# Key masks on VectorE, clears after the first norms, output sums on VectorE or GpSimd, and a planner that counts late instruction blocks

## The chip, the core and the metric

The kernel runs on one core of a Trainium2 chip, as one program. The core has five engines with an instruction queue each: TensorE (PE in the profile), ScalarE (ACT), VectorE (DVE), GpSimd (POOL) and SyncE (SP). The loading of weights into TensorE has a row of its own (PEld). The metric is the device time of one execution in microseconds.

## The reference

Two layers, each made of an attention A and a linear attention B on a residual stream of 2048 tokens by 512, 32 heads of 16. A works in four segments of 512 tokens: causal softmax attention inside a segment, plus a read from a memory that collects the keys and values of earlier segments.

```python
# A, for each segment s
p = softmax(q @ k.T * scale + causal_mask)
a_dot = p @ v
a_mem = (phi(q) @ M) / (phi(q) @ z + 1e-6)      # phi(t) = t+1 if t>0 else exp(t)
o = g * a_mem + (1 - g) * a_dot                 # g = sigmoid(beta), by head
M, z = M + phi(k).T @ v, z + sum(phi(k))
# B, for the whole sequence
phi(t) = concat(softmax(t @ w_phi), softmax(-t @ w_phi))
o = (phi(q) @ (phi(k).T @ v)) / (phi(q) @ sum(phi(k)) + 1e-6)
# twice:
x = x + A(layernorm(x)) @ wo_A
x = x + B(layernorm(x)) @ wo_B
```

## The kernel before

**A recorded program and a planner.** The kernel does not write out its order. Each operation is recorded in a graph with its reads and writes, a planned duration on each engine that may do it, and the tiles that it opens. `forward` then walks through time: whenever an engine is free it takes the ready operation of the highest priority. The result is a fixed order for each engine. Priorities come from twelve backward and forward passes for each of six rules, and then from a list of random moves, `STEPS`, each a seed that shifts the priority of some operations (`moved`). An engine works through its queue strictly in order; each instruction waits on semaphores for what it needs. Durations in the plan are constants in the code; a matmul of c columns is planned at c/2.4 + 2.5 ns.

**The two-engine rule.** Operations marked `port=True` on VectorE are not planned while POOL computes, and POOL does not start while such an operation runs. An operation with two entries in its table, such as `{"dve": (350.0, fn), "pool": (2900.0, fn)}`, may go to either engine.

**Instruction blocks in the plan.** `fetched` counts TensorE's instructions in blocks of `BLOCK = 256` (the first after `FIRST = 193`). Each pair of matmuls counts 4, two weight loads and two matmuls. When the end of a block is reached, the next may be used `FETCH = 3250` ns after the last one began; TensorE is planned to stand until then. The transfers of large inputs are planned one after another at 200 GB/s (`dfree`).

**Start.** `setup` records the loads. Four 128 KB loads of X and the raw weights wq and wk come first; then beta and w_phi on POOL. The loads of wv, of X for tokens 512 to 1023 and of wo are held until the norm of tile 3 (`gate = self.xnop[3]`), the rest (X, w_qkv of B, wo of B) until the norm of tile 7. POOL makes constants and clears: `pP`, the four tiles for diagonal probabilities, are zeroed in part (L879), the last column of the two value tiles `pV` is set to 1 (L881). VectorE clears `pQ2` (L877), held by the gate too. `ln` is the norm: statistics and their sum on VectorE (L918, L919), the inverse root on ScalarE for the first four tiles (L922, L924) and on POOL for the others (L926, L928), and the normed tile on VectorE (L939).

**Projections of A** (`a_proj`). For each half of the heads (`hp`) TensorE makes K and Q in PSUM, ScalarE or VectorE copies them to `KT` and `QT`. The key tile `KD` of `pK` is KT times a mask of 0 and 1 by partition, in two halves (L1028): 2 layers, 4 segments, 2 halves of heads and 2 parts make 32 masks. In the first segment of the first layer the queries too are masked (L1051, tiles `pQ0` and `pQ1`); elsewhere a DMA moves them. wv is scaled by the gate in eight operations on VectorE or POOL (L862, `WA_v`). wq and wk are permuted in sixteen (L871).

**Attention of A** (`a_att`). For each tile of 128 tokens, scores on TensorE (`pQ,pK` and, on the diagonal, `far,II`), exponentials on ScalarE (L651, to `p` and `pP`), products with the values (`pU`, `pV` with `p`, `pP`), division on VectorE (L697, L1173). From the second segment on, the memory part and the softmax part of the output are summed (L1177, 24 sums).

**B.** `b_keys` collects keys, `b_query` makes the output for each tile: a copy by ScalarE, a product with the inverse denominators (L1346, `nmul`), and the sum of the two signs (L1353, 26 sums; the other six tiles sum on TensorE). `out_proj` then transposes the sum by a DMA on SP's queue (`p<-p`), multiplies by wo, adds X on TensorE and copies to X (L659 or L660). In the second layer each tile is stored, from POOL's or SP's queue (L668).

Of the kernel before, what the change touches and what calls it, by code (L numbers as in the profile page):

```python
# [9 lines left out]
ALU = mybir.AluOpType  # L10
# [85 lines left out]
BLOCK, FIRST, FETCH, EXTRA = 256, 193, 3250.0, 0.126  # L96
# [6 lines left out]
class Graph:  # L103
# [143 lines left out]
    def forward(self, prio, pools, rule):  # L247
# [35 lines left out]
        issued, edge, begun = 0.0, float(FIRST), -1e9  # L283

        def fetched(dur, count):
            nonlocal issued, edge, begun
            count += EXTRA
            while issued + count >= edge:
                at = now + dur * (edge - issued) / count
                late = max(0.0, begun + FETCH - at)  # L290
                dur += late
                begun = at + late
                edge += BLOCK
            issued += count
            return dur
# [37 lines left out]
        while len(order) < n + fillers:  # L333
            while ev and ev[0][0] <= now + 1e-9:
                _, kind, i = heapq.heappop(ev)
                o = ops[i]
# [268 lines left out]
class Kernel:  # L605
# [402 lines left out]
    def a_proj(self, L, s):  # L1008
# [6 lines left out]
        for hp in range(2):  # L1015
# [8 lines left out]
            for m in range(2):  # L1024
                def fn(e, KT=KT, KD=KD, m=m, raw=raw):
                    dst = KD.t[:].rearrange("p (t x c) -> p t x c", x=4, c=64)
                    dst = dst[:, :, 0::3] if m else dst[:, :, 1:3]
                    return e.tensor_scalar(dst, KT.t[:].rearrange("p (t x c) -> p t x c", x=2, c=64), self.MK[:, 0 if raw else 1, m:m + 1], None, op0=ALU.mult)  # L1028
                self.g.op({"dve": (350.0, fn), "pool": (2900.0, fn)}, [KT, R("MK0") if raw else R("MK1")], [KD[m]], label="KD", port=True)
# [88 lines left out]
    def a_att(self, L, s, i):  # L1118
# [57 lines left out]
        if s >= 1:  # L1176
            v(lambda e: e.tensor_tensor(o.t[:], o.t[:], tmp.t[:], ALU.add), 335, [o[0], o[1], tmp[0], tmp[1]], [o[0], o[1]], label="oadd", port=True)  # L1177
# [113 lines left out]
    def b_query(self, L, c, store):  # L1291
# [38 lines left out]
        for tt in range(4):  # L1330
# [20 lines left out]
            if not pair:  # L1351
                half = lambda Tm, k: Tm.t[:].rearrange("p (b s c) -> p b s c", b=2, s=2)[:, :, k]
                v(lambda e, Tm=Tm, o=o, half=half: e.tensor_tensor(o.t[:].rearrange("p (b c) -> p b c", b=2), half(Tm, 0), half(Tm, 1), ALU.add),  # L1353
                  335, [Tm], [o], label="nadd", port=True)
# [3 lines left out]
    def build(self):  # L1358
# [9 lines left out]
        for L in range(2):  # L1368
            if L == 0:
                lnA(0, 0)  # L1370
                gate = self.xnop[3]
                for o in self.loads[self.early:self.second] + list(self.pQ.init.values()):
                    o.deps.add(gate)
# [44 lines left out]
def basep(ap):  # L1418
# [17 lines left out]
    1030000018, 1030000077, 1030000092, 1030000099, 1030000166, 1030000168, 1030000222, 1030000289, 1030000308,  # L1436
    1030000326, 1030000342, 1030000389, 1030000420, 1030000560, 1030000645, 1030000784, 1030000851, 1030000966,
    1030000984, 1030001009, 1030001690, 1030002205, 1030002291, 1030002301, 1030002323, 1030002439, 1030002527,
    1030002554, 1030002594, 1030002678, 1030002767, 1030002827, 1030002858, 1030003072, 1030003159, 1030003333,
    1030003714, 1030004121, 1030004204, 1030004671, 1030004934, 1030005425, 1030005496, 1030005653, 1030005764,  # L1440
    1030005994, 1030006207, 1030006544, 1030006744, 1030007011, 1030007046, 1030007069, 1030007218, 1030007220,
    1030007536, 1030008641, 1030008687, 1030008730, 1030009186, 1030009359, 1030009713, 1030009775, 1030009783,
    1030009816, 1030010053, 1030010635, 1030010656, 1030011598, 1030011826, 1030012430, 1030012462, 1030013373,
    1030013471, 1030013815, 1030014294, 1030014816, 1030014962, 1030015673, 1030017494, 1030017518, 1030017657,
    1030018904, 1030019905, 1030022035, 1030200092, 1030200096, 1030200172, 1030200329, 1030200464, 1030200971,
    1030201489, 1030201640, 1030202974, 1030203521, 1000400311, 1000402731, 1000403746, 1000404182, 1010600052,
    1010600600, 1010600903, 1010602519, 1010603776, 1010603875, 1020801005, 1020801937, 1020803898, 1031000849,
    1031002190, 1031003326, 1031004518, 1031201021, 1031202491, 1031202719, 1031202940, 1021400652, 1021400802,
    1021401184, 1021401558, 1021401865, 1021402577, 1021402781, 1021402889, 1021402967, 1021403407, 1031600163,
    1031601117, 1031601674, 1031601919, 1031602223, 1031602684, 1031602829, 1011800463, 1011801166, 1011801985,  # L1450
    1011802229, 1022000655, 1022002114, 1022002161, 1022002512, 1022002519, 1022002841, 1032201850, 1032202263,
    1032202919, 1012400450, 1012400549, 1012400881, 1012401973, 1012802802, 1013002895, 1013202988, 1033401154,
    1033403481, 1023603166, 1033803193, 1004001904, 1004003605, 1004400376, 1004400634, 1004600426, 1004601442,
    1034803444, 1025000113, 1025000301, 1025000392, 1025000954, 1025001054, 1025002108, 1035201603, 1035202380,
    1025601217, 1025601345, 1005800575, 1036000223, 1036001385, 1036002574, 1036201585, 1036201657, 1026401420,
    1016600059, 1016600512, 1016600897, 1016601902, 1036800336, 1036800865, 1036800917, 1036801080, 1036801719,
    1036801832, 1036802798, 1017001663, 1017002043, 1017002740,
# [41 lines left out]
```

## Time and profile before

| what | value |
|---|---|
| median of four runs | 531.06 us (528.14, 530.99, 531.13, 531.29) |
| the profiled run | 528.14 us; its span, first to last instruction, 526.4 us |
| TensorE clock granted, mean | 0.990 |
| key masks L1028 on POOL | 21, median 2862 ns, 62.0 us |
| key masks L1028 on VectorE | 11, median 478 ns, 5.2 us |
| sums L1177 and L1353 on VectorE | 24 of 418 ns and 26 of 414 ns, 20.8 us |
| POOL's inverse roots L926 and L928 | 60 of 338 ns and 60 of 602 ns |
| idle of POOL before L926, for the statistics L919 | 291.0 us |

Busy times of engines overlap, so they do not add up to the span. A clock below 1 means that TensorE was granted fewer cycles. "Idle before, releaser" names what ended an engine's wait. L640 is the line of the helper that issues nearly all matmuls, L651 that of ScalarE's operations: there one goes by the tiles. DMA transposes of a tile are issued on SP's queue and take 2.7 us (median) from issue to landing.

### The profile page before, as it was taken

Reading aid. Unit: us, or ns where it says so; the run is one execution under the profiler, and the core shown is the slowest. Engines: PE = TensorE matmul, PEld = TensorE weight load, DVE = VectorE, ACT = ScalarE, POOL = GpSimd, SP = SyncE. Lnnn points to the kernel's source line nnn. Section 1 sums busy time; section 2 is a strip of 40 time slices with the busy share of each in tenths; the row PEclk is TensorE's granted clock in tenths of the full one; section 3 lists DMA queues with packets and bytes.
Section 4 is the critical chain, followed back from the end, with each engine's and each line's share of the span. In section 5 each row is a group of like instructions: output and inputs, shape, how many; then the busy total and the mean of one; then the engine's idle time right before and its main releaser. Section 6 shows DMA issues by size and latency. Waiting matters only on the chain.

```text
span 526.4 us, 26401 instructions
## 1 busy us (share of the span) xinstructions
PE 474.9 (90%) x12182; PEld 320.9 (61%) x12182; DVE 423.7 (80%) x851; ACT 446.3 (85%) x555; POOL 144.0 (27%) x198
## 2 busy tenths in 40 slices
PE   7975998899989899999898989998989989999896
PEld 3353765565667676555756666665666656665674
DVE  6983899889978976886989879888887797877771
ACT  4784999889889899876998889999889998877894
POOL 6870571050450010000342281720041000010022
PEclk9997899999999999999999999999999999999999
DMA  6259345515223032000044445353112211100366
GB/s 191 52 148 199 64 92 92 92 37 92 44 39 70 14 44 34 12 2 2 21 66 103 92 101 97 77 74 59 33 34 54 54 23 33 24 14 2 44 137 128
DMA packets 90335, 34.11 MB, mean 65 GB/s; under 512 B 76752, under 2 KB 89072, under 8 KB 90224
## 3 DMA queue, kind: packets, MB, share of 16 engines
q1 hardware_dynamic: 88624, 27.68, 28.6%
q0 software_dynamic: 1600, 4.74, 3.1%
q8 instruction: 95, 1.56, 1.3%
q14 instruction: 16, 0.13, 0.1%
HBM read 6.32 MB, written 2.10 MB: 16 GB/s over the span
## 4 chain that ended last, share of the span: by engine, by line
PE 56%; ACT 18%; DMA 10%; DVE 10%; issue 3%; POOL 2%; SPq 0%; DVEq 0%
PE D L640 56%; ACT p L651 11%; DMA p<-p 7%; ACT pP L651 4%; POOL pK L1028 2%; DMA pX<-p 2%; DVE pT L1271 1%; DMA pK<-in_A_wv_dram 1%; DVE p L1173 1%; DVE X L1206 1%; DVE p L660 1%; DVE stats L918 1%; DVE pS L1251 1%; ACT X L659 1%; DMA X<-in_A_x_dram 1%
## 5 line engine op out<-in xcount | busy, mean ns | idle before, releaser
L651 ACT ACTIVATE p<-D 128x1024 bf16<-128x1024 f32 (+1 forms) x292 | 284.4, 1021 | 37.5 <-PE D L640 35.1
L640 PE MATMUL D<-pQ,pK 64*128 64x256 bf16 (+1 forms) x1356 | 118.3, 262 | 13.0 <-ACT pP L651 4.3
L651 ACT ACTIVATE pP<-D 128x768 bf16<-128x768 f32 x128 | 101.5, 822 | 15.1 <-PE D L640 13.8
L926 POOL TENSOR_SCALAR rstd<-mv 128x1 f32<-128x1 f32 x60 | 20.2, 338 | 291.0 <-DVE mv L919 291.0
L640 PEld LDWEIGHTS D<-pQ,pK 64*128 64x128 bf16 x1356 | 56.4, 94 | 51.2 <-ACT p L651 9.8
L1028 POOL TENSOR_SCALAR pK<-p,MK 128x1024 bf16<-128x1024 bf16 x21 | 62.0, 2958 | 34.9 <-DVE p L660 24.9
L640 PE MATMUL D<-pV,p 64*128 64x34 bf16 (+1 forms) x1736 | 66.7, 180 | 1.0 <-issue 0.9
L640 PE MATMUL D<-pU,p 64*128 64x34 bf16 x1536 | 59.3, 176 | 4.6 <-issue 4.0
L640 PEld LDWEIGHTS D<-pV,p 64*128 64x128 bf16 x1736 | 49.8, 93 | 5.8 <-issue 5.0
L640 PE MATMUL D<-pU,pP 64*128 64x34 bf16 x1024 | 49.6, 176 | 0.4
L640 PE MATMUL D<-pV,pP 64*128 64x34 bf16 x1024 | 49.5, 175 | 0.0
L640 PEld LDWEIGHTS D<-pU,p 64*128 64x128 bf16 x1536 | 45.8, 93 | 5.4 <-PE D L640 0.8
L1173 DVE TENSOR_TENSOR p<-D,pS 128x256 bf16<-128x256 f32 x112 | 46.9, 421 | 2.5
L1251 DVE TENSOR_REDUCE pS<-p 128x64 f32<-128x1024 bf16 (+1 forms) x36 | 38.8, 1090 | 10.8 <-ACT p L651 10.6
L640 PE MATMUL D<-WB_o,p 64*128 64x256 bf16 x512 | 38.0, 270 | 8.1 <-DMA p<-p 6.4
L918 DVE BATCH_NORM_STATS2 stats<-X 128x6 f32<-128x512 bf16 x64 | 43.4, 686 | 2.1 <-DMA X<-in_A_x_dram 1.1
L640 PE MATMUL D<-WA_o,p 64*128 64x256 bf16 x518 | 39.3, 270 | 5.0 <-DMA p<-p 3.2
L1271 DVE TENSOR_TENSOR pT<-D,pT 128x1024 bf16<-128x1024 f32 x32 | 38.8, 1218 | 3.3 <-PE D L640 3.0
L697 DVE RECIPROCAL pS<-D 128x32 f32<-128x32 f32 (+1 forms) x64 | 20.9, 327 | 20.9 <-PE D L640 20.5
L660 DVE CAST p<-D 128x1024 bf16<-128x1024 f32 (+2 forms) x33 | 34.6, 1069 | 3.7 <-PE D L640 2.9
L640 PE MATMUL D<-WB_k,pX 64*128 64x512 bf16 (+1 forms) x288 | 33.8, 352 | 4.0 <-DMA pX<-p 2.0
L640 PE MATMUL D<-far,II 64*128 64x256 bf16 x256 | 35.7, 272 | 1.8 <-issue 1.8
(130 smaller groups left out, 938.2 us busy)
## 6 DMA issues: line engine op xcount, KB each, us to landing
pQ<-p SPq DMA_DIRECT2D x28, 128.0 KB, 2.2
pU<-pV SPq DMA_DIRECT2D x32, 68.0 KB, 2.3
out_dram<-X POOLq DMA_DIRECT2D x13, 128.0 KB, 2.8
pX<-in_B_wqkv_dram POOLq DMA_DIRECT2D x3, 512.0 KB, 8.4
p<-p SPq DMA_TRANSPOSE x76, 2.7
X<-in_A_x_dram SPq DMA_DIRECT2D x2, 512.0 KB, 8.0
pX<-p SPq DMA_TRANSPOSE x54, 2.5
X<-in_A_x_dram SPq DMA_DIRECT2D x4, 128.0 KB, 2.9
```

Of the source, the lines that this page charges most:

```text
L640: ins = e.matmul(out_ap, lhsT, rhs, start=st, stop=sp, tile_position=(basep(lhsT), 0))
L651: return self.g.op({"act": (dur, lambda e: e.activation(out_ap(), in_ap(), func, scale=scale))}, reads, writes, opens, label=label)
L659: ch = {"act": (slow or n / 1.2 + 51, lambda e: e.activation(out_ap(), in_ap(), ACT.Copy)), "dve": ((340 if fast else n / 0.96 + 65), lamb ...
L660: "dve": ((340 if fast else n / 0.96 + 65), lambda e: e.tensor_copy(out_ap(), in_ap()))}
L697: return e.reciprocal(o, i)
L918: v(lambda e: e.bn_stats(self.stats[:, t, :], self.X[:, t, :]), 602, [R("X", t)], [R("st", t)], label="bn")
L926: v(lambda e: e.tensor_scalar(rs, self.mv[:, t, 1:2], LN_EPS, None, op0=ALU.add), 240, [R("mv", t)], [R("rstd", t)], eng="pool", label="rstd")
L1028: return e.tensor_scalar(dst, KT.t[:].rearrange("p (t x c) -> p t x c", x=2, c=64), self.MK[:, 0 if raw else 1, m:m + 1], None, op0=ALU.mult)
L1173: v(lambda e, pvv=pvv, rden=rden, part=part, dst=dst, k=k: e.tensor_tensor(part(dst), pvv()[:, :, k, :, 0:16], rden()[:, :, k, :, None].to ...
L1206: self.v(lambda e: e.tensor_tensor(xt(), xt(), res(), ALU.add), 602, [R("X", t), ps], [R("X", t)], label="res")
L1251: fn = lambda e, sgn=sgn, ev=ev, Z=Z, nz=nz: e.tensor_reduce(Z.t[:, sgn * nz:(sgn + 1) * nz], ev().rearrange("p (h d) -> p h d", d=16), AX ...
L1271: v(lambda e, Vt=Vt, src=src, vt=vt: e.tensor_tensor(vt(Vt, 0, 16), src(), vt(Vt, 16, 17).to_broadcast([128, 2, 2, 2, 16, 8]), ALU.mult), ...
```

## The change

Five edits, of which the last follows from the others:

- A key mask may run on VectorE only.
- The sums L1177 and L1353 may run on VectorE or POOL, planned at 335 and 1150 ns.
- The clears of `pP` and `pV` are held by the norm of tile 3, as those of `pQ` were.
- `fetched` plans a later block: it may be used `FETCH` after the end of the one before, or later, up to `SLOW` = 7500 ns after it, while planned transfers of inputs end later than that (2300 ns after their end, `BEHIND`).
- `STEPS`, the list of random moves, is replaced by another.

```diff
-BLOCK, FIRST, FETCH, EXTRA = 256, 193, 3250.0, 0.126
+
+BLOCK, FIRST, FETCH, EXTRA, SLOW, BEHIND = 256, 193, 3250.0, 0.126, 7500.0, 2300.0
...
-        issued, edge, begun = 0.0, float(FIRST), -1e9
+        issued, edge, usable = 0.0, float(FIRST), 0.0
 
         def fetched(dur, count):
-            nonlocal issued, edge, begun
+            nonlocal issued, edge, usable
             count += EXTRA
             while issued + count >= edge:
                 at = now + dur * (edge - issued) / count
-                late = max(0.0, begun + FETCH - at)
+                late = max(0.0, usable - at)
                 dur += late
-                begun = at + late
+                at += late
+                usable = max(at + FETCH, min(at + SLOW, max(dfree.values()) + BEHIND))
                 edge += BLOCK
             issued += count
             return dur
...
-                self.g.op({"dve": (350.0, fn), "pool": (2900.0, fn)}, [KT, R("MK0") if raw else R("MK1")], [KD[m]], label="KD", port=True)
+                self.g.op({"dve": (350.0, fn)}, [KT, R("MK0") if raw else R("MK1")], [KD[m]], label="KD", port=True)
...
-            v(lambda e: e.tensor_tensor(o.t[:], o.t[:], tmp.t[:], ALU.add), 335, [o[0], o[1], tmp[0], tmp[1]], [o[0], o[1]], label="oadd", port=True)
+            fn = lambda e: e.tensor_tensor(o.t[:], o.t[:], tmp.t[:], ALU.add)
+            self.g.op({"dve": (335.0, fn), "pool": (1150.0, fn)}, [o[0], o[1], tmp[0], tmp[1]], [o[0], o[1]], label="oadd", port=True)
...
-              v(lambda e, Tm=Tm, o=o, half=half: e.tensor_tensor(o.t[:].rearrange("p (b c) -> p b c", b=2), half(Tm, 0), half(Tm, 1), ALU.add),
-                  335, [Tm], [o], label="nadd", port=True)
+                fn = lambda e, Tm=Tm, o=o, half=half: e.tensor_tensor(o.t[:].rearrange("p (b c) -> p b c", b=2), half(Tm, 0), half(Tm, 1), ALU.add)
+                self.g.op({"dve": (335.0, fn), "pool": (1150.0, fn)}, [Tm], [o], label="nadd", port=True)
...
-                for o in self.loads[self.early:self.second] + list(self.pQ.init.values()):
+                for o in self.loads[self.early:self.second] + [o for p in (self.pQ, self.pP, self.pV) for o in p.init.values()]:
                     o.deps.add(gate)
...
 STEPS = (
-    1030000018, 1030000077, 1030000092, 1030000099, 1030000166, 1030000168, 1030000222, 1030000289, 1030000308,
+    1130000000, 1130000008, 1130000026, 1130000130, 1130000135, 1130000150, 1130000183, 1130000236, 1130000245,
...
```

Because the plan is made anew, the order of all engines differs. Counted in the two orders: all 32 key masks stand on VectorE; of the 50 sums 44 stand on POOL; of the last 14 sums 11 are on POOL; of the 16 stores POOL issues 10 (13 before) and SP 6 (3 before); of the sixteen permutations of wq and wk ScalarE does 13 and VectorE 3 (16 and none before); five of the eight scalings of wv are on VectorE and three on POOL (6 and 2 before). Matmuls are 12136 (12184 before).

## The prediction

> **What bounds the kernel now.** I read the page first (shares of the engines, the 40 slices), then the chain of waits from 6 to 60 us, then the timeline there, then a table of stretches.
>
> ```profile
> span 526.4 us, 26401 instructions
> ...
> PE 474.9 (90%) x12182; PEld 320.9 (61%) x12182; DVE 423.7 (80%) x851; ACT 446.3 (85%) x555; POOL 144.0 (27%) x198
> ...
> PE   7975998899989899999898989998989989999896
> DMA  6259345515223032000044445353112211100366
> ...
> PE 56%; ACT 18%; DMA 10%; DVE 10%; issue 3%; POOL 2%; SPq 0%; DVEq 0%
> ```
>
> TensorE is busy 90% of the span and its matmuls stay, so time can only come out of the 51.5 us in which it stands. The second line of digits (PE) is low in the first five slices of 13.2 us and in the last one. The chain of the first 60 us says why:
>
> ```profile
> 8.65 0.33 DVE p L939
> ...
> 9.27 7.00 DMA pK<-in_A_wv_dram
> ...
> 16.34 1.63 POOL WA_v L862 x2
> 17.97 9.63 POOL pK L1028 x3
> 27.60 0.72 POOL rstd L928
> ...
> 28.41 0.90 PE D L640 x14
> ...
> 39.58 1.83 issue
> ...
> 46.60 4.01 issue
> ```
>
> The first norm (L939) releases the load of wv at 9.27; it takes 7.00 us; three key masks on POOL (9.63 us) stand until 27.60, and the first scores start at 28.41. Later TensorE stops twice on "issue", which is a wait for nothing that the profile shows, 1.83 and 4.01 us.
>
> ```profile
> 6.38 1.07 POOL L879 MEMSET pP<- 128x256 bf16 x4
> ...
> 6.56 1.50 DVE L848 TENSOR_SCALAR gt<-gt 128x32 f32<-128x32 f32 x1
> ...
> 7.37 0.66 POOL L881 MEMSET pV<- 128x128 bf16 x1
> ...
> 27.08 1.98 DVE L1051 TENSOR_SCALAR pQ<-p,MQ 128x1024 bf16<-128x1024 bf16 x4
> ```
>
> Here a VectorE operation of 32 numbers takes 1.50 us and ends (8.06) as POOL's clears end (8.03). And the last thing that the first scores need is not POOL's mask but the second query mask on VectorE, which ends near 28.07 (half of the 1.98 us).
>
> ```profile
> 30.00:40.00 10.00, 7.98 (x219) 5.26 (x214) 7.62 (x17) 10.00 (x13) 6.86 (x12) 1.00 0.69 181
> 40.00:50.00 10.00, 5.19 (x127) 3.50 (x128) 2.78 (x6) 4.86 (x7) 0.00 (x0) 0.77 1.29 216
> 50.00:60.00 10.00, 8.95 (x233) 6.50 (x234) 6.76 (x19) 6.38 (x8) 4.31 (x11) 0.71 0.42 85
> ```
>
> Columns: stretch, its length, busy PE, PEld, DVE, ACT, POOL, granted clock, DMA share, GB/s. Both stops lie where weights are loading (DMA share 1.29), and the clock falls to 0.77 and 0.71: 14.1 us of TensorE work at about 0.74 cost near 3.7 us more. The early loss from stops and clock is 5.8 + 3.7 = 9.5 us.
>
> **What the Trainium skill says.** "SBUF — State Buffer", section "Who interferes with whom": POOL and VectorE share a port pair, and whichever comes second fully waits; the 1.50 us above agrees. "Runtime: NRT & Kernel Launch", section "Instruction fetch mechanics": instructions come in blocks of 256 by a DMA queue of the engine's own, mostly hidden. The trace agrees with the block (q8: 95 packets, 1.56 MB) and not with the hiding: counted in the order of instructions, TensorE stops at matmul 480 and 608, which are 128 matmuls, or 256 instructions with their weight loads, apart. "TensorE: Matmul & The Clock Gate", Part 1: an idle window of about 3.4 us halves the clock; the drop after the 4.01 us stop agrees. For a price, "GPSIMD Engine Reference", section 3.1: a two-input add costs about 2.6 cycles an element.
>
> **The change part by part.** The order of instructions, before and changed, gives the counts.
>
> *First clears behind the first norms.* Four pP and two pV clears leave the place at 6.38 us and come after the issue of wv. VectorE's first two norms now follow the fourth statistics at 6.56 at once, so the norm ends near 7.2 and wv is issued 2.1 us earlier than 9.27. It then shares the DMAs with the end of the raw query and key weights; I leave 0.6 of it there and take wv landed 1.5 us earlier, near 14.8 (bounds 0 and 2.1). The same 1.7 us of clears now hold VectorE around 8 to 10 us; there it waits for w_phi anyway (issued at 4.63, 5.1 us to land); uncovered, the projections would start up to 1.4 us later, but wv is still the later of the two.
>
> *Key masks on VectorE.* 21 masks of 2.96 us leave POOL; 21 x 0.48 = 10.1 us come to VectorE. At the start, between wv and the second query mask, VectorE's new order has five WA_v (3.80/6 each, 3.2), three statistics (2.0 with one aggregate), two casts out of PSUM (2.3), two key masks (1.0), two weight permutations (not on VectorE before; between a third and all of ScalarE's 0.62: take 0.4, so 0.8) and two query masks (1.0): 10.3 us. Before it was 28.07 - 16.29 = 11.8. So 1.5 us, with wv 3.0 us together: first scores near 25.4. ScalarE was idle 1.91 us just before its first exponential and then full to 40 us, so an earlier start is kept; three of its permutations (0.62 each) have also gone to VectorE. Elsewhere TensorE waits for POOL 1.7 us in total, so masks later on win nothing directly.
>
> *Output sums on either engine.* 44 of 50 leave VectorE (44 x 0.42 = 18.5 us). POOL's price is not in the trace: its two-input WA_v of 256 elements takes 0.83, twice that is 1.67; the skill gives 512 x 2.6 / 1.2 GHz = 1.1 us. I take 1.3, that is 57 us, in the place of 62 us of masks. VectorE's net is 10.1 - 18.5 = -8.4 us; as it holds 10% of the chain, I count -0.8 (bounds 0 and -3). Each sum is later by 0.9 us; hidden where other tiles are ready, not at the end.
>
> *Late blocks.* Only the planner changes: it now lets a block arrive up to 7.5 us after its request while loads are queued. It removes no transfer; it moves work. In the new order the second wave of loads hangs on the first of the four next norms, estimated at 29.2 us instead of 32.87, and the last 512 KB of it waits for the weight permutations. At the 200 GB/s of those stretches 2.5 MB end near 42 and the rest near 44 to 45; before, the loads filled the queues to about 49. Matmul 480 is still reached under full queues: I take 3 us of stop there (1.8 to 5). Block 608 is asked for near 39 to 40 and needed 5.2 us later as before (41.41 to 46.60), when loads end: 0.5 us (0 to 4). That is 3.5 for 5.8; with no stop over 3.4 us I take half of the clock loss, 1.8. Together -4.1, say -4.0 (bounds 0 and -9.5).
>
> *The end.* The last stretch is worked off by transposes on SP's queue (9 in 15.67 us). Before, POOL held 13 stores with nothing behind. Now POOL has 11 of the 14 last sums between its 10 stores, and SP 6 stores, five of them ahead of transposes. A store that waits for its tile holds the sum or transpose behind it. I take +1.5 (0 to +5).
>
> *Matmuls.* The counts that differ (more repeats and fillers, fewer transposes) come to +1392 columns, two halves at once, at 2.4 columns per ns (12 of 512 took 1.47 us): +0.3.
>
> Sum: -3.0 - 4.0 - 0.8 + 1.5 + 0.3 = -6.0 us. The profiled run took 528.14 (span 526.4 and 1.74 around it), so 522.1 against it. The other three runs took 531.0 to 531.3 and the median is 531.06; carried over, 525.0. The new order of all other work can move this by some 3 us either way; I take nothing for it.
>
> **Rivals.**
> *Stops eat the start.* TensorE reaches 480 three us earlier while the loads start 3.7 us earlier too: the block is no earlier in need, and the stops grow by what the start gains. For it: both stops are bound to DMA. Against: the loads end earlier. It leaves -3.0 + 1.5 = -1.5: 529.5.
> *Queues block (slower).* One mechanism: in the end stretch, in-order POOL and SP queues, ten stores ahead of sums and transposes. The plan in the code counts 2.6 us for a transpose from issue to landing; the chain has 4.51, 4.16 and 4.83 there, so each store comes ready 2 us later than planned and holds what is behind. Half of them in sequence are 10 us for my 1.5. From 7.5 us (four stores in sequence) it eats the 6.0; at 10 it is 531.06 - 7.5 + 10 = 533.6, and with the 44 slow sums ahead of the norms' roots on POOL about 535. Against: two of SP's stores follow one another, and other sums are ready meanwhile.
> *Stops vanish.* The whole 9.5 goes: -3.0 - 9.5 - 0.8 + 1.5 + 0.3 = -11.5: 519.6. For it: the loads are spread; against: 480 lies in their midst.
>
> **How the numbers follow.** Forecast 0.46 (its own range 521 to 529), stops eat the start 0.16, queues block 0.22, stops vanish 0.16. 0.5% is 2.7 us, about what a measurement can tell from no change: below 528.4 lie 0.39 of the forecast, 0.05 of the first rival and all of the last, 0.60; between 528.4 and 533.7, 0.07 + 0.11 + 0.04 = 0.22; above, 0.18. A range from 518 to 534 leaves out most of the slow rival and a little below.
>
> **What would show it.** wv issued near 7.2 and landed near 14.8; no 1.50 us on L848's row; first scores near 25.4 (28 or later: the start is wrong). Stops of "issue" of some 3.5 us between 30 and 60 and a clock above 0.74 there. VectorE's busy time near 415, POOL's near 140. In the last 30 us, POOL's sums behind stores that wait for X: more than 3 us of it and the forecast is too low.

## The result, and the profile after

The changed kernel takes 534.07 us (median of 37 runs), the kernel before 529.98 (58 runs on the same chip); the ratio is 1.0053 with an interval of [1.0035, 1.0071]. The forecast was 525.0. A second comparison, on another chip, gave 1.0078 [1.0048, 1.0108]. So the change costs about half a per cent to three quarters, some 3 to 4 us. (Medians are over all runs and ratios leave disturbed runs out, so that the two can differ a little.)

The profiled run of the changed kernel took 534.24 us, with a span of 532.5, which is 6.1 more than that of before. This pair differs by more than the typical runs do, so sizes read from it are checked below in other profiles. The page of the changed kernel:

```profile
span 532.5 us, 26294 instructions
...
PE 477.4 (90%) x12134; PEld 321.7 (60%) x12134; DVE 424.0 (80%) x830; ACT 445.2 (84%) x552; POOL 131.0 (25%) x217
...
PE   7977989889889998999889989989999988999885
...
DMA  8098445242211121000145564125412122000375
...
PE 54%; ACT 18%; DVE 11%; DMA 10%; issue 3%; SPq 2%; POOL 1%
```

TensorE's busy time is 2.5 us more (477.4 for 474.9), its idle time 532.5 - 477.4 = 55.1 us for 51.5. VectorE's busy time has not fallen. On the chain, SPq, which was 0%, has 2%. The chain of waits in the first 60 us (start, duration, what):

```profile
7.00 6.37 DMA pK<-in_A_wv_dram
...
13.39 3.06 DVE WA_v L864 x5
...
37.75 1.06 issue
...
46.23 0.52 issue
```

wv is issued at 7.00 instead of 9.27 and is there at 13.36 instead of 16.27; the waits on "issue" are 1.06 and 0.52 us on the chain. The timeline of VectorE and POOL in the same stretch (start, duration, engine, line):

```profile
6.71 0.15 DVE L850 TENSOR_SCALAR gt<-gt 128x32 f32<-128x32 f32 x1
...
7.77 1.09 POOL L881 MEMSET pP<- 128x256 bf16 x4
8.78 1.20 POOL L883 MEMSET pV<- 128x128 bf16 x2
...
22.00 0.88 DVE L1053 TENSOR_SCALAR pQ<-p,MQ 128x1024 bf16<-128x1024 bf16 x2
```

The 32-number operation (L850 now) takes 0.15 us where it took 1.50, since the clears follow the issue of wv (it takes 0.15 us too in `b_clears` below, where only the clears are moved); the two query masks end near 22.9 and the first scores start at 22.94, 5.5 us earlier than before. All this came as forecast, or better. In a second profile of the changed kernel wv is there at 14.96 and the first scores start at 24.5. The stretches that held the stops (columns as before: stretch, length, busy PE, PEld, DVE, ACT, POOL, granted clock, DMA share, GB/s):

```profile
30.00:40.00 10.00, 7.67 (x224) 5.28 (x218) 8.49 (x22) 10.00 (x16) 3.46 (x7) 0.93 1.20 275
40.00:50.00 10.00, 7.18 (x114) 4.50 (x112) 5.89 (x16) 6.44 (x9) 3.98 (x11) 0.67 1.04 162
50.00:60.00 10.00, 10.00 (x225) 6.68 (x222) 8.32 (x20) 9.03 (x11) 2.97 (x8) 0.89 0.31 68
```

Between 40 and 50 us TensorE still stands for 2.8 us, and the clock still falls, to 0.67, under a DMA share above 1. The second stop is longer than the 0.52 us of the chain, which runs over ScalarE up to 46.23. In the timeline of TensorE and of its weight loads (in brackets the idle time before, and what ended it):

```profile
46.74 1.89 PE L642 MATMUL D<-pX,WA_k 64*128 64x512 bf16 x8 [2.47 <-ACT p L653]
...
46.71 0.16 PEld L642 LDWEIGHTS D<-pX,WA_k 64*128 64x128 bf16 x4 [2.72 <-issue]
```

Both end at 46.7: the stop took 2.47 us of TensorE, 2.72 of the loads, and with the 1.06 before it TensorE lost 3.5 us, where it had lost 5.8. The forecast was 3.5 us as well, but by luck: it had 3 us for the first stop, which took 1.06, and 0.5 for the second, which took 2.47. And the second one is not shown to be a late block. The row of the matmuls names ScalarE (L653), only the row of the loads names nothing. The second profile has a stop of 2.12 us at the same matmul; there ScalarE works until 47.45 and TensorE goes on at 47.62. So most of this stop, if not all, may be a wait for ScalarE, and the waits on "issue" alone are 1.06 and 0.52 us on the chain.

To find where the time went I cut both spans at the same pieces of work. "Rkv" is the product of the finished memory of B on VectorE (L1224 before, L1227 after), which opens the queries of B. Each cell gives the length and, after the stroke, TensorE's idle time in it; "changed, again" is the profile of a second run of the same kernel, on another chip.

| up to | before | changed | changed, again |
|---|---|---|---|
| first scores | 28.4 / 5.8 | 22.9 / 4.5 | 24.5 / 5.2 |
| 60 us | 31.6 / 7.9 | 37.1 / 6.0 | 35.5 / 6.8 |
| last attention tile, layer 0 | 167.6 / 12.3 | 164.7 / 15.7 | 164.0 / 14.0 |
| Rkv, layer 0 | 15.8 / 0.3 | 17.5 / 0.4 | 17.5 / 0.4 |
| 44th X tile written | 185.7 / 14.9 | 190.8 / 14.8 | 190.9 / 16.2 |
| 48th (last attention tile, layer 1) | 42.6 / 2.5 | 36.6 / 2.4 | 37.2 / 2.9 |
| Rkv, layer 1 | 15.0 / 0.2 | 18.7 / 0.2 | 18.7 / 0.2 |
| end | 39.7 / 7.7 | 44.2 / 11.1 | 43.5 / 10.3 |

Three things stand out. The first scores are 5.5 us earlier (3.9 in the second profile), but TensorE's idle time ahead of them is only 1.3 us less (0.6). In the attention of layer 0 TensorE idles 3.4 us more (1.7), which is what the first 60 us saved (3.2 and 1.7). And behind the last Rkv product the changed kernel takes 4 to 4.5 us longer, with some 3 us more of idle time. The windows of the last three stages, first of the kernel before, then of the changed one:

```profile
429.10:471.70 42.60, 40.10 (x1121) 28.18 (x1120) 34.51 (x64) 36.37 (x42) 3.15 (x8) 1.00 0.14 25
471.70:486.70 15.00, 14.84 (x208) 8.00 (x206) 10.74 (x17) 11.72 (x13) 0.79 (x2) 1.00 0.01 2
486.70:526.40 39.70, 32.01 (x902) 24.14 (x896) 22.77 (x55) 28.95 (x50) 7.13 (x13) 1.00 0.53 102
```

```profile
433.00:469.60 36.60, 34.16 (x1006) 23.50 (x1008) 27.11 (x49) 32.67 (x38) 6.59 (x11) 1.00 0.17 25
469.60:488.30 18.70, 18.49 (x298) 11.28 (x294) 14.18 (x22) 12.33 (x15) 0.79 (x2) 1.00 0.01 3
488.30:532.50 44.20, 33.14 (x918) 25.13 (x914) 24.06 (x45) 30.68 (x52) 19.97 (x21) 1.00 0.48 92
```

The reader is to see the last line of each: POOL has 13 us more to do there, TensorE 1.1 us more, and the stretch is 4.5 us longer. In the stage before it TensorE is full in both, with 298 recorded matmuls for 208: that is work which the four attention tiles before it, done in 36.6 us for 42.6, had left undone. The chain of the changed kernel in the last stretch:

```profile
493.27 1.16 POOL p L1356
...
494.45 3.71 DMA p<-p
...
498.21 0.98 PE D L642 x26
...
507.56 1.16 POOL p L1356
...
508.73 4.24 DMA p<-p
...
519.02 0.34 SPq L670
...
519.40 0.43 SPq L670
...
519.87 1.20 SPq L666
...
521.17 1.21 SPq L666
...
522.42 4.66 DMA p<-p
```

Sums on POOL (L1356, 1.16 us each) lie on the chain twice, and near the end two stores (L670) and two issues of transposes (1.20 and 1.21) follow one another on SP's queue, 3.2 us, which is less than half of SPq's 2% of the chain. This is what the rival "Queues block" had described, and 534.07 lies in its range. The experiments say how much of it is the cause.

### The profile page after: what moved, and what is told of

Read it like the earlier page. It is cut to its first block, busy times and chain, and to the rows that moved or that the text cites. A ratio compares the mean times of both kernels' runs of the same rounds, so it can differ in the third digit from the quotient of the medians.

```text
span 532.5 us, 26294 instructions
## 1 busy us (share of the span) xinstructions
PE 477.4 (90%) x12134; PEld 321.7 (60%) x12134; DVE 424.0 (80%) x830; ACT 445.2 (84%) x552; POOL 131.0 (25%) x217
## 3 DMA queue, kind: packets, MB, share of 16 engines
q1 hardware_dynamic: 89216, 28.20, 28.7%
## 4 chain that ended last, share of the span: by engine, by line
PE 54%; ACT 18%; DVE 11%; DMA 10%; issue 3%; SPq 2%; POOL 1%
PE D L642 54%; ACT p L653 12%; DMA p<-p 5%; ACT pP L653 4%; SPq L666 2%; DVE p L1175 2%; DMA pX<-p 1%; DVE p L1349 1%; DVE stats L920 1%; DMA pK<-in_A_wv_dram 1%; DVE X L1209 1%; ACT p L661 1%; DVE pT L1274 1%; DMA pX<-pX 1%; DVE pS L699 1%
## 5 line engine op out<-in xcount | busy, mean ns | idle before, releaser
L653 ACT ACTIVATE p<-D 128x1024 bf16<-128x1024 f32 (+1 forms) x292 | 284.8, 1017 | 48.7 <-PE D L642 45.4
L642 PE MATMUL D<-pQ,pK 64*128 64x256 bf16 (+1 forms) x1334 | 120.0, 264 | 10.7 <-ACT p L653 5.3
L653 ACT ACTIVATE pP<-D 128x768 bf16<-128x768 f32 x128 | 101.8, 821 | 10.5 <-PE D L642 9.4
L928 POOL TENSOR_SCALAR rstd<-mv 128x1 f32<-128x1 f32 x60 | 15.8, 265 | 183.8 <-DVE mv L921 183.6
L1179 POOL TENSOR_TENSOR p<-p 128x512 bf16<-128x512 bf16 x23 | 28.2, 1227 | 92.7 <-DVE p L1175 92.7
L642 PEld LDWEIGHTS D<-pU,p 64*128 64x128 bf16 x1536 | 44.3, 93 | 6.9 <-PE D L642 1.0
L1356 POOL TENSOR_TENSOR p<-p 128x512 bf16<-128x512 bf16 x21 | 26.8, 1276 | 81.7 <-DVE p L1349 81.6
L920 DVE BATCH_NORM_STATS2 stats<-X 128x6 f32<-128x512 bf16 x64 | 43.5, 685 | 1.7 <-ACT X L661 0.8
L642 PE MATMUL D<-WA_o,p 64*128 64x256 bf16 x534 | 40.9, 272 | 4.1 <-DMA p<-p 2.7
L642 PE MATMUL D<-WB_k,pX 64*128 64x512 bf16 (+1 forms) x288 | 35.1, 360 | 10.0 <-issue 6.3
L930 POOL TENSOR_TENSOR rstd<-rstd,mhalf 128x1 f32<-128x1 f32 x60 | 35.4, 592 | 4.6
```

Source lines behind the costliest of these rows:

```text
L642: ins = e.matmul(out_ap, lhsT, rhs, start=st, stop=sp, tile_position=(basep(lhsT), 0))
L653: return self.g.op({"act": (dur, lambda e: e.activation(out_ap(), in_ap(), func, scale=scale))}, reads, writes, opens, label=label)
L920: v(lambda e: e.bn_stats(self.stats[:, t, :], self.X[:, t, :]), 602, [R("X", t)], [R("st", t)], label="bn")
L928: v(lambda e: e.tensor_scalar(rs, self.mv[:, t, 1:2], LN_EPS, None, op0=ALU.add), 240, [R("mv", t)], [R("rstd", t)], eng="pool", label="rstd")
L930: v(lambda e: e.tensor_tensor(rs, rs, self.mhalf[:], ALU.pow), 560, [R("rstd", t), R("mhalf")], [R("rstd", t)], eng="pool", label="rstd")
L1179: fn = lambda e: e.tensor_tensor(o.t[:], o.t[:], tmp.t[:], ALU.add)
```

## The experiments

In the first two groups the plan is made first, as the kernel's code makes it, and then the listed orders of the engines (`self.g.order`) are edited; nothing else moves, unless stated. Ratios are to the kernel before, run on the same chip. Most rest on 14 to 22 executions of the edited kernel, that of `a_same` on nine, those of `h_ba` and `h_amid8` on six.

**1. Back in the changed order: sums, stores, masks.** `a_sums` puts layer 1's output sums back on VectorE at their places in the order; `a_both` also moves four of SP's stores to POOL; `a_masks` returns three of the first four key masks to POOL. `b_sums` does the reverse in the kernel before: 11 of its last 14 sums go to POOL. The comments in the cut say which run has which lines; the edit that notes a sum's layer is left out.

```diff
+        for o in self.g.order:                              # a_sums, a_both
+            if o.label == "nadd" and o.eng == "pool" and o.layer == 1:
+                o.eng = "dve"
+        for o in self.g.order:                              # a_both
+            if o.label == "store" and o.eng == "sp" and "pool" in o.ch:
+                o.eng = "pool"
...
+        tail = [o for o in self.g.order if o.label == "nadd" and o.layer == 1]      # b_sums
+        for n, o in enumerate(tail):
+            if n not in (5, 8, 12):
+                o.ch["pool"] = o.ch["dve"]
+                o.eng = "pool"
...
+        masks = [o for o in self.g.order if o.label == "KD"][:4]                    # a_masks
+        for n, o in enumerate(masks):
+            if n != 3:
+                o.ch["pool"] = o.ch["dve"]
+                o.eng = "pool"
```

> The changed kernel with its order kept; only the second layer's output sums of B (L1356) that it puts on POOL, 11 of them in the last 40 us, are done by VectorE at the same place of the order. Theory T (the last stretch: sums of 1.15 us and more on POOL, behind stores in POOL's queue, make SP's transposes late): the time from the second Rkv product to the end falls from 44 us to about 40.5, the ratio to the kernel before from 1.005 to about 0.999. Rival R (the new order leaves more TensorE work for the end, 3.7 us between the last attention tile and the last keys, whoever sums): no more than 1 us, ratio 1.003 to 1.005.

> As the run before it, and besides the stores that the changed kernel issues from SP's queue between transposes go to POOL, at the same place of the order, four of them, so that SP issues only transposes until the end and POOL only stores. Theory T: another 1 to 2 us, ratio about 0.996, and below the kernel before in any case. Rival R: as without it, 1.003 to 1.005.

> The kernel before with its order kept; 11 of the 14 last output sums (all but the 6th, 9th and 13th) are done by POOL at the same place of the order, between its stores. Theory T: slower by 3 to 4 us, ratio 1.006 to 1.008, all of it after 490 us. Rival R: within 1 us, ratio 0.998 to 1.002.

> The changed kernel with its order kept; three of the four key masks of the first segment go back to POOL (2.9 us each), at the same place. If the early start of the scores (22.9 us against 28.4 before) is carried to the end, as theory T takes it, the first scores move to about 26 and the end is later by 2 to 3 us: ratio 1.009 to 1.011. If the start is swallowed by stops for instruction blocks or later waits, the end stays: ratio 1.004 to 1.006.

Measured: `a_sums` 1.0080 [1.0056, 1.0103], `a_both` 1.0069 [1.0038, 1.0099], `b_sums` 1.0007 [0.9981, 1.0034], `a_masks` 1.0075 [1.0045, 1.0104]. Theory T came true in none of the first three. In the profile of `a_sums` the stretch behind the last Rkv is 42.1 us, some 2 less than in the changed kernel, but no gain is to be seen in the ratio; and in the old order the same sums on POOL cost nothing that can be measured. So the engines of the sums and stores, taken by themselves, do not make the loss. And with the masks back on POOL the time is no different from that of the changed kernel either, though the first scores then start at 25.3; the interval reaches from one expectation of `a_masks` to the other, so this run does not say whether the earlier start lasts to the end.

**2. The parts of the change in the old order.** `b_clears` moves the clears of pP and pV behind the issue of wv; `b_masks` puts all 21 POOL masks on VectorE; `b_feat` does both and moves the first two query masks up behind the first two key masks (the edit for this is not shown). `a_same` is the changed kernel, unedited.

```diff
+        order = self.g.order                                # b_clears, b_feat
+        clears = [o for o in order if o.eng == "pool" and o.label in ("zero", "one")]
+        rest = [o for o in order if o not in clears]
+        at = next(n for n, o in enumerate(rest) if o.label == "load" and o.eng == "pool" and o.kb == 512)
+        self.g.order = rest[:at + 1] + clears + rest[at + 1:]
...
+        for o in self.g.order:                              # b_masks, b_feat
+            if o.label == "KD":
+                o.eng = "dve"
```

> The changed kernel once more, on the same chip as the next three, so that they have a baseline of their own. The first comparison gave 1.0053 [1.0035, 1.0071]; on this chip 1.003 to 1.009 is expected by every theory.

> The kernel before, its order kept, with one part of the change: the clears of pP and pV follow the issue of the wv load on GpSimd. Theory O (the parts of the change cost nothing, the newly planned order of the other work does): wv issued near 7.1 instead of 8.6 us, ratio 0.997 to 1.001, for first scores that the order leaves at 28 us. Rival F (the parts themselves cost): above 1.003, from clears that now meet VectorE's or the loads' first work.

> The kernel before, its order kept, with one part of the change: the 21 key masks that GpSimd did are done on VectorE at the same place. Theory O: first scores earlier by the 1.5 us of the first two masks or not at all, VectorE busy +8 us where it has idle time, ratio 0.997 to 1.001. Rival F (VectorE, loaded with the masks, makes TensorE wait in the attention of layer 0, where the changed kernel's idle time grew by 3.4 us): ratio 1.003 to 1.010 and TensorE idle between 60 us and the last attention tile of layer 0 at 15 us instead of 12.3.

> The kernel before with both parts (clears behind the wv load, all key masks on VectorE) and the first two query masks moved up behind the first two key masks, the rest of the order kept. Theory O: first scores at 24 to 26 us instead of 28.4, and a ratio of 0.994 to 1.000, since no other work moves. Rival F: 1.003 or more, with the same idle time of TensorE in layer 0 as the changed kernel. A third reading (the start is worth nothing, since what TensorE does before the first scores is only moved): first scores earlier and ratio 0.999 to 1.001.

Measured: `a_same` 1.0078 [1.0048, 1.0108], `b_clears` 0.9996 [0.9967, 1.0025], `b_masks` 1.0044 [1.0019, 1.0069], `b_feat` 0.9996 [0.9970, 1.0021]. `b_masks` alone is what rival F expected; but its idle time between 60 us and the last attention tile of layer 0 is 11.3 us, not 15, and `b_feat`, which has the same masks on VectorE, is no slower. So clears, key masks and query masks together, in the old order, neither gain nor lose more than 0.3%. Why the masks alone lose is not settled: `b_feat` is faster than `b_masks` by about 0.5%, although its first scores are only 0.8 us earlier (26.6 for 27.3) and TensorE's idle time before them is the same (3.7 and 3.6 us). In `b_feat` the start is 1.8 us earlier than before, less than was expected (24 to 26 us). Its chain of waits says why:

```profile
16.77 1.92 PE D L640 x16
...
20.70 1.92 PE D L640 x16
...
24.63 1.04 PE D L640 x8
25.66 1.08 PE D L996 x10
26.74 0.73 PE D L640 x14
```

With wv and the masks early, TensorE itself is what the first scores wait for: a row of projections, one behind the other, and at its end 1.08 us of fillers (L996, matmuls without a use, which the plan puts into gaps and which keep their place in the order). The idle time up to there is 3.7 us for 5.8; that is all that was to be had in this order, and not even these 2.1 us show in the ratio.

**3. The order exchanged in halves.** Now the two plans are spliced. The operations are the same 2715 in both, so one list can be followed up to a point and the other for all that is left; each engine then takes its operations strictly in the spliced order, and the planner only places buffers, TensorE's fillers and its repeats.

```diff
-        self.g.schedule(self.pools, ROUNDS, OFF)
+        self.g.link()
+        self.g.log = []
+        self.g.replay(self.pools, PLAN)
...
                     if o.eng is not None:
                         continue
+                    if self.force[e][-1] != i:
+                        skipped.append((pr, i))
+                        continue
```

`PLAN` lists operation and engine: `h_ab` is the changed order up to the last Rkv product of layer 0 and the old one behind it; `h_ba` is the old order up to the 20th X tile and the changed one behind it; `h_aend` is the changed order up to the 44th X tile and the old one behind it.

> The changed kernel's order up to the last of layer 0's four Rkv products, the order of the kernel before for all that follows. Theory O1 (the loss lies behind X48, where the new order has more work left and more idle time): 0.998 to 1.001 and some 55 us from X48 to the end, as before, instead of 62.9. Theory O2 (the loss lies in layer 0, where TensorE idles 3.4 us more during the attention): 1.004 to 1.008. If both halves cost alike: 1.002 to 1.005.

> The reverse: the order of the kernel before up to the twentieth X tile written, then the changed kernel's order. Theory O1: 1.004 to 1.008, with 62 to 63 us from X48 to the end. Theory O2: 0.998 to 1.002, with 11 to 12.5 us of idle time on TensorE between 60 us and the last attention tile of layer 0 instead of 14 to 15.7. If both halves cost alike: 1.002 to 1.005.

> The changed kernel's order up to the 44th X tile written, the order of the kernel before for the rest, that is the last four attention tiles of layer 1 and the end. Theory O1: 0.996 to 1.001, X48 near 470 to 472 us and 55 to 57 us from there to the end. Theory O2: 1.004 to 1.008: X48 later by what the end gets shorter.

Measured: `h_ab` 1.0049 [1.0019, 1.0079], `h_ba` 1.0102 [1.0056, 1.0147], `h_aend` 0.9972 [0.9949, 0.9994]. The windows of `h_aend`, for the same three stages as above:

```profile
432.10:473.30 41.20, 39.77 (x1112) 27.81 (x1114) 32.30 (x58) 34.53 (x40) 3.11 (x8) 1.00 0.14 22
473.30:488.30 15.00, 14.84 (x208) 8.03 (x206) 10.71 (x17) 11.72 (x13) 0.79 (x2) 1.00 0.01 2
488.30:528.20 39.90, 32.28 (x902) 24.14 (x898) 22.73 (x55) 29.08 (x50) 7.12 (x13) 1.00 0.47 102
```

From the 44th X tile to the end it takes 41.2 + 15.0 + 39.9 = 96.1 us, against 99.5 in the changed kernel (99.4 in its second profile): 3.4 us less, and TensorE idles 9.2 us there for 13.7. That agrees with the difference of the ratios, 0.8 to 1.1% of 530, in sign, though 3.4 us are 0.64% and so somewhat less. O1 holds for `h_aend`: with the old order from the 44th tile on, the loss is gone. The two splices at the border of the layers decide nothing by themselves, since a splice has a seam: between layer 0's Rkv and the 44th tile `h_ab` takes 190.2 us and `h_ba` 192.3, for 185.7 before and 190.8 in the changed kernel. I take it that layer 0 in one order hands over other work than the other order counts on; no run shows it. `h_ab` has the short end (55.5 us from the 48th tile) and is yet slower than O1 allows; `h_ba` is slower than either theory had it, with 59.6 us from the 48th tile where O1 had 62 to 63. Against O2 speaks `h_ba`: with only 10.3 us of idle time in layer 0's attention it is the slowest of the three.

**4. Which part of the end.** Two more splices of the changed kernel: `h_alast8` takes the old order only behind the last Rkv product; `h_amid8` takes it only between the 44th X tile and that product. `h_aend2` repeats `h_aend` on the same chip.

> The changed kernel's order up to the last of layer 1's four Rkv products, the order of the kernel before only behind it: X48 and Rkv as in the changed kernel (468 to 471 us, 18.7 us apart), but the sums, transposes and stores of the last stretch in the old order and on the old engines. Theory L (the last stretch's own order loses the time): 0.997 to 1.001, with 40 us from the last Rkv to the end instead of 43.5 to 44.2. Theory W (the work that the four tiles before X48 leave undone loses it): 1.004 to 1.008, with 43 us or more.

> The reverse: the changed kernel's order up to the 44th X tile and again behind the last Rkv product, the order of the kernel before between the two. Theory L: 1.004 to 1.009, with 43 us or more from the last Rkv to the end. Theory W: 0.996 to 1.000, with 40 us.

> The kernel with the changed order up to the 44th X tile and the old order behind it once more, on the same chip as these two, as their common baseline. It had 0.9972 [0.9949, 0.9994]; both theories expect 0.995 to 1.000 again, and a value above 1.002 would say that the end stretch was not what the first run showed.

Measured: `h_alast8` 1.0013 [0.9987, 1.0040], `h_amid8` 1.0095 [1.0058, 1.0132], `h_aend2` 0.9973 [0.9946, 1.0000]. `h_amid8` and `h_aend2` differ only behind the last Rkv product, and their intervals lie far apart, as theory L has it; in `h_alast8`, with the old order only there, most of the loss is gone (1.0013, for 1.0053 and 1.0078 on other chips; by the medians over all executions, 531.52 us for 529.11, less of it). `h_alast8` and `h_aend2` differ only between the 44th tile and Rkv, and their intervals overlap: what the undone work costs (W) is some 0.4%, with an uncertainty as large, and stays open. The windows of `h_alast8`:

```profile
433.20:469.90 36.70, 34.24 (x1006) 23.58 (x1008) 27.15 (x51) 32.77 (x38) 6.59 (x11) 1.00 0.15 25
469.90:488.60 18.70, 18.49 (x298) 11.23 (x294) 14.21 (x23) 12.34 (x15) 0.79 (x2) 1.00 0.01 3
488.60:529.50 40.90, 32.33 (x922) 24.82 (x918) 22.87 (x55) 30.29 (x52) 7.12 (x13) 0.99 0.50 99
```

The stage before Rkv is the changed kernel's (18.7 us), the last one is nearly the old one: 40.9 us for 43.5 to 44.2.

But the order of the last stretch is not slow wherever it stands. `h_ba` and `h_amid8` have the same last 194 operations, in the changed order. Their windows behind Rkv, `h_ba` first:

```profile
489.40:530.30 40.90, 32.44 (x946) 25.25 (x942) 24.29 (x45) 30.70 (x52) 19.48 (x21) 1.00 0.44 100
```

```profile
486.10:532.60 46.50, 36.17 (x930) 26.36 (x924) 24.24 (x44) 29.71 (x50) 19.91 (x21) 0.93 0.42 87
```

In `h_ba` the changed order takes 40.9 us with 8.5 us of idle time, no more than the old order in `h_alast8` (40.9 and 8.6), and this kernel loses its time elsewhere. In `h_amid8` TensorE idles 10.3 us, nearly as in the changed kernel, and is busy 3 us longer than there, at a granted clock of 0.93 for 1.00. So the changed order comes with more idle time in the changed kernel and in `h_amid8` and not in `h_ba`: what it costs depends on more than itself, and theory L as a rule of this order alone does not hold.

What differs between the orders is seen in TensorE's timeline. First the kernel before, then the changed one, then `h_alast8`:

```profile
492.21 0.41 PE L640 MATMUL D<-ident,p 64*128 64x64 bf16 x16
...
493.43 0.60 PE L640 MATMUL D<-WB_o,p 64*128 64x256 bf16 x8
```

```profile
498.21 0.61 PE L642 MATMUL D<-WB_o,p 64*128 64x256 bf16 x8 [1.40 <-DMA p<-p]
...
506.93 0.41 PE L642 MATMUL D<-ident,p 64*128 64x64 bf16 x16
```

```profile
495.59 0.41 PE L659 MATMUL D<-ident,p 64*128 64x64 bf16 x16
...
496.79 0.61 PE L659 MATMUL D<-WB_o,p 64*128 64x256 bf16 x8
```

"D<-ident,p" is a transpose on TensorE, which two of the 16 tiles of this stretch have in place of a sum and a transpose by DMA. The old order takes one of them first, and its first product with WB_o comes 6.8 us after Rkv (493.43 - 486.66) and 8.2 us after it in `h_alast8` (496.79 - 488.57). The new order starts with tiles that need a sum (on POOL) and a transpose by DMA, 3.71 us on its chain, and keeps the first of the quick tiles for 506.93: its first product comes 9.9 us after Rkv (498.21 - 488.32), and the second X tile 17.0 us after it, for 14.0 before. This is a difference that goes with the loss, not a cause that was tried: in `h_ba` the changed order has its first product 8.6 us after Rkv (498.01 - 489.42), about as early as `h_alast8`. Whether the order of the tiles or the sequence of stores and transposes on SP is the larger part was not tried separately; the engines alone are not enough, as the first group shows.

## Why the prediction was wrong

*The start, -3.0.* Its events are right: the clears' wait gone, wv 2.9 us earlier (1.3 in the second profile), first scores at 22.94 and 24.5 (forecast 25.4). Its value is not. I took the time at which the first scores start for a gain, because ScalarE then ran full. But up to that point ScalarE has been idle for 11.4 us before and after the change (28.40 - 17.02 before; 22.90 - 11.46 after), and TensorE had used the waiting time for projections. What was saved is idle time of TensorE, 1.3 us (0.6 in the second profile), and the projections came later. `b_feat` has clears and masks of the change in the old order, starts the first scores 1.8 us earlier, and is at 0.9996. (Nor are the first five slices of the page all low, as I read them: three are, 7, 7 and 5, and two are 9.)

*Late blocks, -4.0.* Between the first scores and 60 us TensorE idles 6.0 us for 7.9; the clock's part (busy time times what is missing from 1) is 31.1 x 0.14 = 4.4 us for 23.7 x 0.16 = 3.8. That is -1.3 for -4.0. In the second profile the clock was 0.95 there, which makes it -1.1 for the idle time and 28.7 x 0.05 = 1.4 for the clock, together -3.5; so this term varies from run to run by as much as the change was to bring. The 3.5 us of stops came by luck, as said above: the first was 1.06 us for 3, the second 2.47 for 0.5 with ScalarE named as what ended it. That both stops of the kernel before end a block was counted to matmul 480 and 608; on record they stand at the 477th and the 604th, 127 apart, in the changed kernel at the 478th and the 597th, 119 apart. What failed besides is the other half: I took a better clock from having no stop over 3.4 us, the window of which the Trainium skill, "TensorE: Matmul & The Clock Gate", Part 1, speaks. In this profile the longest stop is 2.47 us, and the clock is 0.67 between 40 and 50 us all the same. The kernel before had shown it already: from 41.4 to 46.6 us, ahead of its stop of 4.01 us and behind one of 1.83, its clock is 0.67.

*VectorE's balance, -0.8.* Counts were right, the sum was not: its busy time is 424.0, not 415. The groups of VectorE, before and after (count, busy, mean ns):

```profile
L1346 DVE TENSOR_TENSOR p<-p,pS 128x1024 bf16<-128x1024 bf16 x32 | 21.7, 686 | 6.3 <-ACT p L651 6.2
...
L1353 DVE TENSOR_TENSOR p<-p 128x512 bf16<-128x512 bf16 x26 | 10.8, 414 | 0.2
...
L1329 DVE TENSOR_TENSOR pS<-pS 128x128 bf16<-128x128 bf16 x8 | 2.3, 283 | 2.7 <-ACT pS L651 2.7
```

```profile
L1349 DVE TENSOR_TENSOR p<-p,pS 128x1024 bf16<-128x1024 bf16 x32 | 23.4, 745 | 3.7 <-ACT p L653 3.5
...
L1332 DVE TENSOR_TENSOR pS<-pS 128x128 bf16<-128x128 bf16 x8 | 4.7, 583 | 3.5 <-ACT pS L653 3.5
...
L1356 DVE TENSOR_TENSOR p<-p 128x512 bf16<-128x512 bf16 x5 | 4.4, 887 | 0.1
```

The 32 masks cost 14.8 us on VectorE for 5.2, and 44 of the 50 sums are gone. Some other work came to VectorE with the new order: it makes 15 copies to X for 10, 10.2 us for 6.8. And L1332 (L1329 before) now takes 583 ns instead of 283, L1349 745 instead of 686, and the five sums that stayed on VectorE in this row 887 instead of 414. These means come from few long ones: three of the eight L1332 take 0.87, 1.14 and 1.24 us and the other five 0.25 to 0.29, and all three overlap a sum on POOL, as in the second profile too. The longest runs from 503.66 to 504.90, while a sum on POOL runs from 503.21 to 504.74; the Trainium skill says why it would ("SBUF — State Buffer", section "Who interferes with whom": a VectorE instruction with two inputs in SBUF, as here, contends with a POOL instruction that reads SBUF). I had priced the sum on POOL (1.3 us; measured 1.23 for L1179 and 1.28 for L1356) and not what it does to VectorE.

*The end, +1.5.* This is the term that was mis-sized most, as far as experiments tell. The stretch behind the last Rkv is 4.5 us longer in the profile, 3.8 in the second one; the exchange of the order from the 44th tile on gives 3.4 back in the profile, and 0.8 to 1.1% (4 to 6 us) in the ratios. I had seen the place (POOL's sums and the stores ahead of transposes on SP) and gave it 1.5 with a bound of +5, and 0.22 of the chance to the rival that prices it at 10. The rival's time (533.6 to 535) is what came; its mechanism is not shown: with sums and stores back on the old engines the time stays. What removes the loss is the old order of this stretch as a whole, its tiles, engines and queues together; `h_ba` shows that the changed order need not lose there. Which part of it loses stays open.

*The new order of all other work, 0 (bounds -3 and 3).* In layer 0's attention TensorE idles 14.0 to 15.7 us for 12.3. That takes back what the start saved: `h_aend` has 14.5 us there, 2.2 more than the kernel before, and 11.2 us up to 60 us, 2.5 less. What in the order makes this idle time was not tried.

With what was measured the sum is -1.3 (start) - 1.3 (to 60 us) + 3.4 (layer 0's attention) + 3.4 (end) = +4.2 for the idle time and the clock of the profiled pair, where the forecast had -6.0; the rest of the 6.1 is busy time of TensorE, whose clock in this profile is 0.98 from layer 0's Rkv to the 44th tile (1.00 before). That the ratios, +3 to +4 us, are near it is chance: in the second profile the same four terms come to -0.6 - 3.5 + 1.7 + 2.6 = +0.2, of a span that is 5.4 us longer. Only the signs hold in both. All of the change but its order from the 44th X tile on has the ratios 0.9972 and 0.9973. That it is faster than the kernel before is not shown: over all executions the medians are 529.08 us for 529.05 in the first comparison and 530.23 for 529.11 in the second. `h_aend` is faster than the changed kernel by about 0.8% (0.9972 by 1.0053, from different chips).

What stays open: how much the new rule for late blocks costs or brings, apart from the search for moves that went with it. The two were not separated, since each rule needs a search of its own. Nor was it tried whether another list of moves, with the same edits, gives a plan with a shorter end: the loss may belong to this one plan and not to the edits.

## What to carry to other kernels

An earlier event is worth at most the idle time that goes with it: before counting the first exponential 5 us earlier as 5 us, look at what the busiest engine did in the wait, and subtract what it now has to do later. When a planner makes the whole order anew, the price of the change is not the sum of its edits; cut both spans at the same pieces of work, do it in more than one profile, and exchange the orders stretch by stretch. One order took 40.9 us in one kernel and 43.5 to 44.2 in another, so a stretch is judged with what runs ahead of it. The engine that a cheap operation moves to has to be priced twice, for itself and for what it does to the neighbour that shares its port.

## What the runs showed of the hardware

- POOL's bf16 sum of 128 x 512 takes 1.23 to 1.28 us; three of VectorE's eight bf16 multiplications of 128 x 128 (L1332) overlap such a sum and take 0.87 to 1.24 us, the other five 0.25 to 0.29 us.
- The granted clock fell to 0.67 between 40 and 50 us in a profile whose longest stop of TensorE there is 2.47 us; in the second profile of the same kernel the mean from the first scores to 60 us is 0.95 instead of 0.86. In the kernel before it was 0.67 from 41.4 to 46.6 us, behind a stop of 1.83 us.
- In the last stretch of `h_amid8` the granted clock was 0.93 and TensorE was busy for 36.2 us, in the changed kernel 1.00 and 33.1 us.
